# A gated attention and maxout kernel: one group of scores transposed instead of computed twice, and a new order in the first sequence's fourth step

## The chip, the cores and the metric

The kernel runs on one core of a Trainium2 chip. TensorE (PE) multiplies matrices and writes to PSUM; VectorE (DVE) and ScalarE (ACT) take results out of PSUM; GpSimd (POOL) and SyncE (SP) issue transfers here, each in its own queue, and both queues share the core's 16 DMA engines. GpSimd's queue carries the loads, SyncE's the transposing transfers between places in SBUF and the stores of the output. Each engine works through its own list of instructions in order and waits on semaphores of the others. The metric is the time on the device in microseconds (us), as a median over runs.

## What is computed

Two functions in a row. The first is an attention without softmax, over 8 sequences of 3072 rows; the second a maxout layer over all 24576 rows.

```python
scores = scale * np.matmul(z, z.transpose(0, 2, 1))     # z: 8 x 3072 x 64
attn = np.maximum(scores, 0.0) ** 2
out = np.matmul(attn, v)                                # v: 8 x 3072 x 256
x = (u * out).reshape(24576, 256)
g = np.maximum(x @ w1, x @ w2)                          # w1, w2: 256 x 1024
y = g @ w_out                                           # w_out: 1024 x 256
```

The score matrix of a sequence is symmetric, since both of its factors are z. The kernel writes the maxout as max(x(w1 - w2), 0) + x w2, so that y = max(x(w1 - w2), 0) w_out + x (w2 w_out); the product w2 w_out is computed once and is called the fold (`fold_w2o`, line 172).

## The kernel before

**Tiles and steps.** The 3072 rows of a sequence are 24 blocks of 128, called k, in 6 groups of four. A step (b, s) makes the 512 output columns of group s of sequence b: it adds up 24 k's in two accumulators of PSUM (`xacc`, one for each half of the 256 values of v), two matmuls of 128x512 for each k (`attn`, line 260). There is one pair of accumulators, so a step can begin only when the `epilogue` (line 264) has taken the accumulators of the step before out of PSUM: VectorE multiplies them with the transposed u (`uT`) and writes xT, two instructions, one for each accumulator.

**Scores.** A score pair (`scores_pair`, line 204) computes two k's against 512 columns: two matmuls of 64x512 on two halves of the array, one Relu on ScalarE into `r_sb`, one square on VectorE into `a_sb`. Three pairs make a window (`scores_window`), whose score matmuls stand together in TensorE's list. Since the scores are symmetric, a block of scores from one step, transposed, serves a later step. `turn` (line 200) sends such a pair through a transposing transfer on SyncE's queue into `aT`; the diagonal group of a step is transposed within itself (`aD`). A k whose scores are a step's own is added by `add_own`, one whose scores came transposed from an earlier step by `add_early`.

**Which scores are computed twice.** `direct(b, i, j)` (line 186) says for which pairs of groups i < j the later step computes the scores itself instead of getting them transposed. Before, this holds in sequence 0 for all of groups 0 to 3. So the steps (0,0) to (0,3) have no transposed rows, and each has 12 pairs of its own.

**Order of the work.** The loop over steps (lines 441 to 495) writes a list `work`. An entry has a nominal time, a mark if it needs the PSUM buffers shared with the scores, a function, and the score tiles that it reads with the time by which they must have been begun. The maxout of a step lags three steps (`LAG`): the hidden layer `put_d` (line 431; four pieces of four matmuls, L74 with tile d_ps) and the output chunk `put_o` (two pieces, tile o_ps) stand in the list of a later step. In step (0,3), the first with such work, the variable `within` puts the hidden layer of step (0,0) ahead of the sixth own pair, and the fold (nominal 1800 ns) with the first output chunk ahead of the tenth. In the steps (0,0) to (0,3) the first and the last four k's are ordered by accumulator (`add_half`): all four for one accumulator, then all four for the other.

**Where the windows go.** Lines 498 to 545 group the tiles to windows and lay them from the last to the first, each at the latest free spot before its tiles are due and at least `GAP_FIRST` or `GAP` before the next window. A spot is free if no entry that shares PSUM ends less than 860 ns before it or begins less than 1700 ns after it.

**Transfers.** Lines 549 to 600 list transfers by a step's nominal begin plus some microseconds: u's load and its transpose (`turn_u`), z and v of the next sequence, the weights. The load of w_out is listed 9 us after the begin of step (0,2). Where a load is reached in the list, GpSimd first runs a `gate` (line 82): a copy of one element of the newest tile (`fresh`), so that the load is not issued before that tile is there. `keep_in_program_order` pins matmuls, SyncE's transfers, gates and loads to the order in which they are written.

Of the kernel before, what the change touches and what calls it, by code (L numbers as in the profile page):

```python
# [11 lines left out]
def kernel(  # L12
# [29 lines left out]
    G = 4  # L42
    WIN = 3
    GW = G * P
    NG = NSB // G
    KD = D // P
    KF = Dff // P
    LAG = 3
    NDIR = 3
# [88 lines left out]
    def make_uT(u_sb):  # L138
        uT = upool.tile([P, G, KD, P], bf16, name="uT")
        sp_dma(  # L140
            out=uT.rearrange("p t c q -> p (t c) q"),
            in_=u_sb.rearrange("p t d -> p (t d)"),
            transpose=True,
        )
        return uT
# [38 lines left out]


    def direct(b, i, j):
        return b == 0 and i < j <= NDIR


    def score(q, out_ps, j, k, s, q0, n):  # L190
# [13 lines left out]
    def scores_pair(b, s, k0):  # L204
        q = seqs[b]
        s_ps = mm_psum.tile([P, 2, GW], fp32, name="s_ps", tag="mm")
        for j in range(2):
            score(q, s_ps[:, j, :], j, k0 + j, s, 0, G)
        yield
        a_sb = apool.tile([P, 2, GW], bf16, name="a_sb")  # L210
        r_sb = apool.tile([P, 2, GW], bf16, name="r_sb", bufs=3)

        head = b == 0 and s == 0 and k0 < 10
        keep = pin if head else lambda ins: None
        if head and k0 in (2, 6):
            keep(nc.vector.tensor_single_scalar(out=r_sb, in_=s_ps, scalar=0.0, op=ALU.max))  # L216
        else:
            keep(nc.scalar.activation(r_sb, s_ps, AF.Relu))  # L218
        if head and k0 < 4:
            yield  # L220
        keep(nc.vector.tensor_mul(a_sb, r_sb, r_sb))  # L221
        gj = k0 // G
        if gj > s and not direct(b, s, gj):
            if (s, gj) not in q.T:
                q.T[s, gj] = tpool.tile([P, G, G, P], bf16, name="aT")
            turn(
                q.T[s, gj][:, ds(k0 - G * gj, 2), :, :].rearrange("p k q x -> p (k q) x"),
                a_sb.rearrange("p j q -> p (j q)"),
            )
        yield a_sb  # L230
# [123 lines left out]
    class Step:  # L354
        def __init__(self, b, s):
            self.b, self.s, self.q = b, s, seqs[b]
            self.xacc = None
            self.n = [0] * KD
            self.diag = not (b == 0 and s <= NDIAG)
            self.rows = ([None] if self.diag else []) + [  # L360
                k0
                for k0 in range(0, NSB, 2)
                if k0 // G > s or direct(b, k0 // G, s) or (k0 // G == s and not self.diag)
            ]
            self.early = [i for i in range(s) if not direct(b, i, s)]
            self.scored = {}
# [11 lines left out]
                self.n[dc] += 1  # L378
            attn(self.q, k, moving, self.xacc, dcs, n == 0, n == NSB - 1)

        def add_early(self, k):
            i, qb = divmod(k, G)
            self.add(k, self.q.T[i, self.s][:, :, qb, :])

        def add_own(self, k, dcs=range(KD)):
            self.add(k, self.scored[k - k % 2][:, k % 2, :], dcs)

        def add_half(self, ks, dc):
            for k in ks:
                self.add_own(k, [dc])  # L390

        def add_diag(self, j):
            self.add(G * self.s + j, self.scored[None][:, j, :, :])
# [26 lines left out]
    LAT_OWN, LAT_TURNED, LAT_DIAG = 2900, 9000, 10000  # L420

    def put(ns, shares, fn, reads=()):
        work.append((ns, shares, fn, reads))

    def put_early(st, ks):
        for k in ks:
            i = k // G
            rows = [((NG * st.b + i, k0), LAT_TURNED) for k0 in (G * st.s, G * st.s + 2)]
            put(432, False, lambda st=st, k=k: st.add_early(k), rows)

    def put_d(n):
        if n >= 0:
            for _ in range(KF // 2):
                put(864, True, steps[n].piece_d)

    def put_o(n, split=False):
        if n >= 0:
            for _ in range(G // 2):
                put(2180, True, lambda: steps[n].piece_o(split))

    for n, st in enumerate(steps):
        b, s = st.b, st.s
        if n:
            put(0, False, steps[n - 1].finish)
        put(0, False, st.begin if n else lambda: None, "begin")
        early = [G * i + j for i in st.early for j in range(G)]

        within = {}
        lat = LAT_OWN if n > LAG else 6 * 432
        if s == 0:  # L450
            put_o(n - LAG)
        elif s == NG - 1:
            put_d(n - LAG)
            put_early(st, early[: len(early) // 2])
            put_o(n - LAG)
            put_d(n - LAG + 1)
            put_early(st, early[len(early) // 2 :])
        elif early:
            put_d(n - LAG)
            put_early(st, early[:-2])  # L460
            put_o(n - LAG)
            put_early(st, early[-2:])
        elif n == LAG:
            within = {
                5: lambda: put_d(0),
                9: lambda: (put(1800, True, fold_w2o), put_o(0)),
            }
        own = [k0 for k0 in st.rows if k0 is not None]
        for i, k0 in enumerate(own):
            if i in within:  # L470
                within[i]()
            if not early and n <= LAG and i in ((0, 1) if n else ()) + (len(own) - 2, len(own) - 1):


                if i in (0, len(own) - 2):
                    ks = [own[i], own[i] + 1, own[i + 1], own[i + 1] + 1]
                    for dc in range(KD):
                        put(
                            864,
                            False,  # L480
                            lambda st=st, ks=ks, dc=dc: st.add_half(ks, dc),
                            [((n, own[i]), lat), ((n, own[i + 1]), lat)],
                        )
                continue
            for k in (k0, k0 + 1):
                put(432, False, lambda st=st, k=k: st.add_own(k), [((n, k0), lat)])
        if st.diag:
            for j in range(G):
                put(432, False, lambda st=st, j=j: st.add_diag(j), [((n, None), LAT_DIAG)])
# [50 lines left out]
    for w in reversed(range(len(windows))):  # L540
        limit = min([limit] + [due[r] for r in windows[w] if r in due])
        found = [i for i in spots if begins[i] <= limit]
        i = found[-1] if found else 0
# [11 lines left out]
    def plan(b, s, us, is_load, fn):  # L555
        transfers.append((start_of[b, s] + us * 1000, len(transfers), is_load, fn))

    def plan_load(b, s, us, fn):
        plan(b, s, us, True, fn)

    def fetch_u(b, s):
        seqs[b].u_sb[s] = load_u(b, s)

    def turn_u(b, s):
        seqs[b].uT[s] = make_uT(seqs[b].u_sb[s])

    def fetch_z(b):
        seqs[b].z_sb = load_z(b, [NSB])
        seqs[b].v = new_v()

    def turn_z(b):
        seqs[b].zT = make_zT(seqs[b].z_sb)

    def fetch_v(b, i):
        load_v(b, seqs[b].v, i * G, G)

    for n, st in enumerate(steps):
        b, s = st.b, st.s
        if n + 1 < len(steps):
            nx = steps[n + 1]  # L580
            plan_load(b, s, 2 if b == 0 else 4, lambda nx=nx: fetch_u(nx.b, nx.s))
        plan(b, s, 1, False, lambda b=b, s=s: turn_u(b, s))
        if s == 0 and b + 1 < B:
            c = b + 1
            if b == 0:
                z_at, zT_at = (3, 5), (4, 4)
                v_at = [(3, 9), (3, 14), (4, 0), (4, 5), (4, 9), (4, 13)]
            else:
                z_at, zT_at = (2, 9), (3, 12)
                v_at = [(3, 2), (3, 8), (3, 14), (4, 2), (4, 8), (4, 14)]  # L590
            plan_load(b, *z_at, lambda c=c: fetch_z(c))
            plan(b, *zT_at, False, lambda c=c: turn_z(c))
            for i, at in enumerate(v_at):
                plan_load(b, *at, lambda c=c, i=i: fetch_v(c, i))
# [89 lines left out]
```

## Time and profile before

| | |
|---|---|
| median of 3 runs | 981.85 us (981.44 to 981.95) |
| the profiled execution's own time | 981.29 us |
| its span, first to last instruction | 979.5 us |
| busy: TensorE matmul, weight loads | 968.7, 510.3 us |
| busy: VectorE, ScalarE, GpSimd | 432.2, 442.6, 77.7 us |
| score matmuls (s_ps), recorded | 696 |
| transposes of score tiles (aT<-a_sb) | 228, median 3.6 us to landing |
| load of w_out | 1, issued at 52.0 us, 7.9 us to landing |
| loads of v and of u | 48 each, median 5.9 and 5.3 us to landing |

The span is shorter than the execution's time by what lies around the program. A line of a group in the profile names the line of the kernel, the engine, the operation, what is written and read, the number of instructions and their durations. All matmuls go through one helper and have line L74, so they are told apart by the tile that they write: s_ps scores, xacc attention, d_ps hidden layer, w2o_ps fold, o_ps output. A matmul of 512 columns shows a duration of 379 ns from its issue to its end, while such matmuls follow each other more closely, since they overlap; a few records of matmuls are missing.

### The profile page before, as it was taken

The numbers are of one execution on the slowest core, as the hardware profiler recorded it, in microseconds if no ns is written. First come the engines' busy times: TensorE is split into PE (matmuls) and PEld (weight loads), VectorE is DVE, ScalarE is ACT, GpSimd is POOL, SyncE is SP. The second block draws the span as 40 slices with busy tenths as digits, with TensorE's granted clock in tenths as the row PEclk, the third lists the DMA queues.
The fourth block names the chain that finished last, engine by engine and source line by source line (L and its number), as shares of the span: only waits on it lengthen the run. The fifth ranks groups of instructions, "written<-read, shape, count | busy, mean of one in ns | idle before, by whom it ended". The sixth has DMA issues, their size and how long they took to land.

```text
span 979.5 us, 14514 instructions
## 1 busy us (share of the span) xinstructions
PE 968.7 (99%) x5662; PEld 510.3 (52%) x5743; DVE 432.2 (44%) x681; ACT 442.6 (45%) x500; POOL 77.7 (8%) x228
## 2 busy tenths in 40 slices
PE   9999999999999999999999999999999999999998
PEld 3355545555455554555545564455545555445556
DVE  6654444443544435433445334444345443554322
ACT  6853454334643355433554335533355433654322
POOL 2011000110001100010000100011000110000000
PEclk9999999999999999999999999999999999999999
DMA  9999599987999969897788979889778796796621
GB/s 151 171 161 187 103 182 150 164 149 123 175 160 144 155 123 177 150 170 128 151 156 144 179 119 157 148 153 181 135 147 149 136 187 127 149 161 118 109 66 65
DMA packets 378517, 143.46 MB, mean 146 GB/s; under 512 B 356944, under 2 KB 358608, under 8 KB 378448
## 3 DMA queue, kind: packets, MB, share of 16 engines
q1 hardware_dynamic: 361888, 112.78, 61.5%
q0 software_dynamic: 16560, 29.74, 21.6%
q8 instruction: 45, 0.74, 0.3%
q14 instruction: 24, 0.20, 0.1%
HBM read 59.77 MB, written 25.17 MB: 87 GB/s over the span
## 4 chain that ended last, share of the span: by engine, by line
PE 99%; issue 1%; DVE 0%; ACT 0%
PE xacc L74 52%; PE o_ps L74 21%; PE d_ps L74 17%; PE s_ps L74 8%; PE w2o_ps L74 0%; ACT r_sb L218 0%; DVE r_sb L216 0%; PE tpz L134 0%; DVE a_sb L221 0%; DVE o_sb L317 0%; DVE blank L333 0%
## 5 line engine op out<-in xcount | busy, mean ns | idle before, releaser
L74 PEld LDWEIGHTS <-v_sb 128*128 128x128 bf16 x2304 | 215.9, 98 | 277.7 <-issue 41.1
L218 ACT ACTIVATE r_sb<-s_ps 128x1024 bf16<-128x1024 f32 x258 | 248.6, 1023 | 111.4 <-PE s_ps L74 111.2
L221 DVE TENSOR_TENSOR a_sb<-r_sb 128x1024 bf16<-128x1024 bf16 x260 | 179.4, 691 | 212.9 <-ACT r_sb L218 208.9
L74 PE MATMUL xacc<-a_sb,v_sb 128*128 128x512 bf16 x997 | 231.3, 379 | 2.5 <-issue 0.2
L74 PE MATMUL xacc<-aT,v_sb 128*128 128x512 bf16 x912 | 216.5, 379 | 0.0
L74 PE MATMUL o_ps<-w_out_sb,g_sb 128*128 128x256 bf16 x1536 | 199.1, 273 | 0.0
L74 PE MATMUL d_ps<-xT,w_sb 128*128 128x512 bf16 x751 | 172.7, 379 | 0.9
L74 PEld LDWEIGHTS <-g_sb 128*128 128x128 bf16 x1536 | 149.9, 98 | 27.6
L292 ACT ACTIVATE g_sb<-d_ps 128x1024 bf16<-128x1024 f32 x96 | 98.3, 1024 | 138.8 <-PE d_ps L74 138.8
L292 DVE TENSOR_SCALAR g_sb<-d_ps 128x1024 bf16<-128x1024 f32 x96 | 117.4, 1223 | 84.7 <-PE d_ps L74 81.3
L323 ACT COPY o_sb<-o_ps 128x512 f32<-128x512 f32 x94 | 55.1, 586 | 178.2 <-PE o_ps L74 178.2
L268 DVE SCALAR_TENSOR_TENSOR xT<-xacc,uT 128x512 bf16<-128x512 f32 x96 | 62.0, 683 | 137.4 <-PE xacc L74 137.4
L74 PEld LDWEIGHTS <-w_sb 128*128 128x128 bf16 x768 | 75.1, 98 | 88.7
L74 PE MATMUL s_ps<-zT 64*128 64x512 bf16 (+3 forms) x696 | 89.2, 359 | 0.1
L246 ACT ACTIVATE r_sb<-s_ps 128x896 bf16<-128x896 f32 x44 | 40.3, 917 | 97.9 <-PE s_ps L74 97.9
L74 PE MATMUL xacc<-aD,v_sb 128*128 128x512 bf16 x331 | 79.9, 379 | 2.6 <-issue 2.2
L74 PE MATMUL o_ps<-W2o_sb,xT 128*128 128x256 bf16 x384 | 73.3, 273 | 0.0
L248 DVE TENSOR_SCALAR r_sb<-s_ps 128x384 bf16<-128x384 f32 x44 | 24.6, 558 | 95.3 <-PE s_ps L74 95.3
L74 PEld LDWEIGHTS <-zT 64*128 64x128 bf16 x696 | 27.3, 94 | 62.6 <-issue 50.5
L83 POOL COPY gate_sb<-g_sb 128x1 bf16<-128x1 bf16 x44 | 8.3, 188 | 407.8 <-DVE g_sb L292 238.5
L74 PEld LDWEIGHTS <-xT 128*128 128x128 bf16 x384 | 37.6, 98 | 4.3
L83 POOL COPY gate_sb<-a_sb 128x1 bf16<-128x1 bf16 x48 | 9.7, 202 | 271.8 <-DVE a_sb L221 271.8
(37 smaller groups left out, 143.3 us busy)
## 6 DMA issues: line engine op xcount, KB each, us to landing
out_dram<-o_sb SPq DMA_DIRECT2D x47, 512.0 KB, 4.1
v_sb<-in_v_dram POOLq DMA_DIRECT2D x48, 256.0 KB, 5.9
u_sb<-in_u_dram POOLq DMA_DIRECT2D x48, 256.0 KB, 5.3
aT<-a_sb SPq DMA_TRANSPOSE x228, 3.6
z_sb<-in_z_dram POOLq DMA_DIRECT2D x7, 384.0 KB, 7.5
aD<-aD SPq DMA_TRANSPOSE x132, 2.4
w_sb<-in_moe_w_dram POOLq DMA_DIRECT2D x2, 512.0 KB, 7.5
uT<-u_sb SPq DMA_TRANSPOSE x48, 4.3
```

Source lines behind the costliest of these rows:

```text
L74: pin(nc.tensor.matmul(*args, **kw))
L83: pin(nc.gpsimd.tensor_copy(gate_sb, tile_ap))
L218: keep(nc.scalar.activation(r_sb, s_ps, AF.Relu))
L221: keep(nc.vector.tensor_mul(a_sb, r_sb, r_sb))
L246: nc.scalar.activation(r_sb, s_ps[:, 0:7, :], AF.Relu)
L248: nc.vector.tensor_single_scalar(out=r2_sb, in_=s2_ps[:, 2:5, :], scalar=0.0, op=ALU.max)
L268: nc.vector.scalar_tensor_tensor(out=xT[:, dc, :].rearrange("p (t q) -> p t q", q=P), in0=xacc[dc].rearrange("p (t q) -> p t q", q=P), sca ...
L292: nc.any.tensor_single_scalar(out=g_sb[:, nb : nb + 2, :], in_=d_ps, scalar=0.0, op=ALU.max)
L323: nc.any.tensor_copy(o_sb[:, ds(2 * th, 2), :], o_ps[:, :, :D])
```

## The change

`direct` gets a third condition, j - i < 3, which excludes the one case i = 0, j = 3. Step (0,0) now transposes its pairs 12, 13 and 14, 15 by DMA, and step (0,3) reads its first four k's from these instead of computing the pairs 0, 1 and 2, 3.

Step (0,3) so has transposed rows and takes the form of the later steps: hidden layer of step (0,0), all transposed rows but two, fold, output chunk of step (0,0), last two transposed rows, own rows. `within` is gone. The order by accumulator stays at the first four k's of steps (0,1) and (0,2) and at the last four of steps (0,0) and (0,1).

The transposes of u for steps (0,1) to (0,3) are listed 3 us ahead of the step's nominal begin instead of 1 us after it. The six loads of v for sequence 1 are listed from 6 us into step (0,4) to 11 us into step (0,5), instead of from 9 us into step (0,3) to 13 us into step (0,4). The other transfers are listed as before.

```diff
--- before.py
+++ after.py
@@ -184,7 +184,7 @@
 
 
     def direct(b, i, j):
-        return b == 0 and i < j <= NDIR
+        return b == 0 and i < j <= NDIR and j - i < 3
 
 
     def score(q, out_ps, j, k, s, q0, n):
@@ -378,16 +378,16 @@
                 self.n[dc] += 1
             attn(self.q, k, moving, self.xacc, dcs, n == 0, n == NSB - 1)
 
-        def add_early(self, k):
+        def add_early(self, k, dcs=range(KD)):
             i, qb = divmod(k, G)
-            self.add(k, self.q.T[i, self.s][:, :, qb, :])
+            self.add(k, self.q.T[i, self.s][:, :, qb, :], dcs)
 
         def add_own(self, k, dcs=range(KD)):
             self.add(k, self.scored[k - k % 2][:, k % 2, :], dcs)
 
         def add_half(self, ks, dc):
             for k in ks:
-                self.add_own(k, [dc])
+                (self.add_early if k // G in self.early else self.add_own)(k, [dc])
 
         def add_diag(self, j):
             self.add(G * self.s + j, self.scored[None][:, j, :, :])
@@ -422,11 +422,22 @@
     def put(ns, shares, fn, reads=()):
         work.append((ns, shares, fn, reads))
 
+    def reads_of(st, k, lat):
+        n, i = NG * st.b + st.s, k // G
+        if i in st.early:
+            return [((n - st.s + i, k0), LAT_TURNED) for k0 in (G * st.s, G * st.s + 2)]
+        return [((n, k - k % 2), lat)]
+
     def put_early(st, ks):
         for k in ks:
-            i = k // G
-            rows = [((NG * st.b + i, k0), LAT_TURNED) for k0 in (G * st.s, G * st.s + 2)]
-            put(432, False, lambda st=st, k=k: st.add_early(k), rows)
+            put(432, False, lambda k=k: st.add_early(k), reads_of(st, k, 0))
+
+
+
+    def put_border(st, ks, lat):
+        reads = sum((reads_of(st, k, lat) for k in ks), [])
+        for dc in range(KD):
+            put(864, False, lambda dc=dc: st.add_half(ks, dc), reads)
 
     def put_d(n):
         if n >= 0:
@@ -444,9 +455,9 @@
             put(0, False, steps[n - 1].finish)
         put(0, False, st.begin if n else lambda: None, "begin")
         early = [G * i + j for i in st.early for j in range(G)]
-
-        within = {}
+        own = [k for k0 in st.rows if k0 is not None for k in (k0, k0 + 1)]
         lat = LAT_OWN if n > LAG else 6 * 432
+
         if s == 0:
             put_o(n - LAG)
         elif s == NG - 1:
@@ -455,35 +466,24 @@
             put_o(n - LAG)
             put_d(n - LAG + 1)
             put_early(st, early[len(early) // 2 :])
-        elif early:
+        elif n >= LAG:
             put_d(n - LAG)
             put_early(st, early[:-2])
+            if n == LAG:
+                put(1800, True, fold_w2o)
             put_o(n - LAG)
             put_early(st, early[-2:])
-        elif n == LAG:
-            within = {
-                5: lambda: put_d(0),
-                9: lambda: (put(1800, True, fold_w2o), put_o(0)),
-            }
-        own = [k0 for k0 in st.rows if k0 is not None]
-        for i, k0 in enumerate(own):
-            if i in within:
-                within[i]()
-            if not early and n <= LAG and i in ((0, 1) if n else ()) + (len(own) - 2, len(own) - 1):
-
-
-                if i in (0, len(own) - 2):
-                    ks = [own[i], own[i] + 1, own[i + 1], own[i + 1] + 1]
-                    for dc in range(KD):
-                        put(
-                            864,
-                            False,
-                            lambda st=st, ks=ks, dc=dc: st.add_half(ks, dc),
-                            [((n, own[i]), lat), ((n, own[i + 1]), lat)],
-                        )
-                continue
-            for k in (k0, k0 + 1):
-                put(432, False, lambda st=st, k=k: st.add_own(k), [((n, k0), lat)])
+        else:
+            ks = (early + own)[:G] if n else []
+            if ks:
+                put_border(st, ks, lat)
+            early, own = early[G:], own[len(ks) if not early else 0 :]
+            put_early(st, early)
+        tail = own[-G:] if n + 1 < LAG else []
+        for k in own[: len(own) - len(tail)]:
+            put(432, False, lambda st=st, k=k: st.add_own(k), reads_of(st, k, lat))
+        if tail:
+            put_border(st, tail, lat)
         if st.diag:
             for j in range(G):
                 put(432, False, lambda st=st, j=j: st.add_diag(j), [((n, None), LAT_DIAG)])
@@ -579,12 +579,12 @@
         if n + 1 < len(steps):
             nx = steps[n + 1]
             plan_load(b, s, 2 if b == 0 else 4, lambda nx=nx: fetch_u(nx.b, nx.s))
-        plan(b, s, 1, False, lambda b=b, s=s: turn_u(b, s))
+        plan(b, s, -3 if b == 0 and 0 < s <= LAG else 1, False, lambda b=b, s=s: turn_u(b, s))
         if s == 0 and b + 1 < B:
             c = b + 1
             if b == 0:
                 z_at, zT_at = (3, 5), (4, 4)
-                v_at = [(3, 9), (3, 14), (4, 0), (4, 5), (4, 9), (4, 13)]
+                v_at = [(4, 6), (4, 11), (4, 16), (5, 1), (5, 6), (5, 11)]
             else:
                 z_at, zT_at = (2, 9), (3, 12)
                 v_at = [(3, 2), (3, 8), (3, 14), (4, 2), (4, 8), (4, 14)]
```

## The prediction

> **What bounds the kernel now.** I read the page first (busy shares, granted clock, chain of what ended last), then busy time by stretches of the span, then the chain between 44 and 80 us, where the change reorders the work, then the tile that is loaded there, and last the timeline for the two engines that decide when it arrives.
>
> ```profile
> span 979.5 us, 14514 instructions
> PE 968.7 (99%) x5662; PEld 510.3 (52%) x5743; DVE 432.2 (44%) x681; ACT 442.6 (45%) x500; POOL 77.7 (8%) x228
> PEclk9999999999999999999999999999999999999999
> PE 99%; issue 1%; DVE 0%; ACT 0%
> ```
>
> TensorE is busy all the time at full clock and nearly the whole chain is TensorE. So a saving off TensorE is worth nothing, a matmul taken away is worth its own time, and every microsecond that TensorE must wait is lost for good: no later slack gives it back. By stretches (us, then busy time of PE, PEld, DVE, ACT, POOL, then clock, share of the DMA engines, GB/s) the early part looks like the rest:
>
> ```profile
> 47.00:50.60 3.60, 3.60 (x21) 1.33 (x22) 3.49 (x5) 2.85 (x3) 0.00 (x0) 1.00 1.09 216
> 50.60:54.00 3.40, 3.35 (x18) 1.28 (x18) 2.91 (x6) 2.85 (x3) 1.08 (x2) 1.00 1.22 171
> 54.00:60.00 6.00, 6.00 (x32) 2.60 (x32) 3.90 (x5) 4.57 (x5) 1.69 (x6) 1.00 1.42 178
> ```
>
> TensorE has no hole, but the DMA engines are at or above full share, so transfers here land late. The chain through this stretch (start, length, what):
>
> ```profile
> 47.20 0.75 PE s_ps L74 x6
> 47.95 2.70 PE xacc L74 x12
> 50.65 0.75 PE s_ps L74 x6
> ...
> 56.69 3.45 PE d_ps L74 x16
> 60.14 1.73 PE xacc L74 x8
> ...
> 64.45 1.75 PE w2o_ps L74 x16
> 66.20 4.37 PE o_ps L74 x40
> ```
>
> Here a window of three score pairs and the 12 matmuls between two windows alternate every 3.45 us. Step (0,3) starts at about 50.6. The first step's hidden layer (d_ps) comes 6 us into it, the fold of the output weights (w2o_ps) at 64.3 to 64.5, the first output chunk behind that. The fold's operand (answer for w_out_sb):
>
> ```profile
> L74 PE MATMUL w2o_ps<-w_out_sb,w2T_sb x16: 272/272/273, 64.3 to 65.9; 128*128 128x256 bf16 x16
> L86 POOL DMA_DIRECT2D w_out_sb<-in_moe_w_out_dram x1: 894/894/894, 52.0 to 52.0; - x1
> DMA to landing us min/median/max: 7.9/7.9/7.9
> ```
>
> It is issued at 52.0, lands at 59.9 and is first read at 64.3: a slack of 4.4 us. What holds its issue is the gate on GpSimd, a copy that waits for the newest score tile (timeline):
>
> ```profile
> 50.74 0.68 DVE L221 TENSOR_TENSOR a_sb<-r_sb 128x1024 bf16<-128x1024 bf16 x1
> 51.56 0.18 POOL L83 COPY gate_sb<-a_sb 128x1 bf16<-128x1 bf16 x1 [9.49 <-DVE a_sb L221]
> 52.02 0.89 POOL L86 DMA_DIRECT2D w_out_sb<-in_moe_w_out_dram  x1 [0.28 <-issue]
> ```
>
> **The change, part by part.**
>
> *Scores removed.* Step (0,3) no longer computes pairs k 0, 1 and 2, 3: four score matmuls, two Relu, two squares. A period of 3.45 us holds 12 matmuls of 0.2157 (the 16 d_ps in 3.45 us) and three pairs, that is 4 x 0.2157. Laying the tiles out by the kernel's rule, 346 instead of 348, still gives 117 windows, so what a window costs beyond its pairs stays; two pairs at 0.2157 go: **-0.43 us**, on the path. The Relus (2 x 1.02) and squares (2 x 0.69) ran beside matmuls: 0.
>
> *Two transposes added on SP* in step (0,0), tiles (12, 13) and (14, 15), behind u's transpose, which is issued at 15.0 and lands at 21.8 (6.8 us). Their squares are ready about 15.0 and 15.9. Four such transposes took 9.94 us of SP from 16.87 to 26.81; six at that rate take 15, to about 31.3; by the 1.3 us of an issue that is not held up, to about 26. The next tile SP needs is ready at 30.4, so the queue is at most 1 us late there. Cover: these two tiles are wanted only in step (0,3), 54 us. u's transpose is ahead of them in its queue; its reader starts at 22.54 and the accumulator is wanted at 23.73, so it may be 1.2 us late before TensorE waits. I take 0; bounds 0 and 1.
>
> *u's transposes sooner.* Between old and new place of those of steps 1, 2 and 3 no other transposes are issued (the windows there hold tiles that are not turned), so SP issues in the same order. SP is in order and waits for u's load, which landed at 19.4, 32.1 and 46.6, earlier than SP gets there (26.9, 40.6, 52.1). Taken as 0; if u came late, the score transposes behind it would be late by as much.
>
> *v of the next sequence later*, on GpSimd behind its gates: six loads with 5.9 us to landing, moved from steps 3 and 4 to steps 4 and 5. The last is listed 9.5 us of list time ahead of sequence 1 and used 21 us after that begin; the first groups have longer. u's loads keep their order but for being passed by a v load of 0.5 us issue. 0; if the cover went, each late group would cost its lateness.
>
> *The order in step (0,3).* This is the part that counts. Before, step (0,3) had no transposed rows and put the hidden layer after ten k's, the fold after eighteen. Now it takes the common form: hidden layer (16 matmuls), k 0 and 1 (4 matmuls), fold, output chunk, k 2 and 3, own rows. No score window may lie in that stretch by the planner's 860/1700 rule. Up to the last matmul of step (0,2), at 50.58, TensorE has the same list as before. So the fold is reached at 50.58 + 16 x 0.2157 + 4 x 0.2157 = **54.9**, which is 9.4 us earlier than the 64.3 of before. Its other operands are there: w1's difference at 48.9, the transposed w2 at 48.6, the transposed scores long before.
>
> The load of w_out is not moved: still 9 us of list time into step (0,2), behind the same gate. 9.4 us sooner against a slack of 4.4: about 5.0 us late. Finer: the gate waits for the third square of the last window of step (0,2). Its Relu ends at 50.41, so the square can't end before 51.1 (issue 51.7); with the accumulators of (0,2) now finishing together, one evacuation of 0.68 ahead of it gives issue at 52.5, two 53.2. Landing: 7.9; the other two loads of that size (w1, w2) have a mean of 7.5, with 6.2 and 8.8 as ends. Ends of the stall: 51.7 + 6.2 - 54.9 = 3.0, and 52.5 + 8.8 - 54.9 = 6.4. I take one evacuation at half weight: 52.2 + 7.9 - 54.9 = **+5.2 us**. Behind the fold in TensorE's order stand the output chunk (which reads w_out too) and all else, so nothing fills the hole. Delays of k 0, of PSUM slots or of hidden-layer evictions vanish within it.
>
> The Trainium skill prices a GpSimd DMA lower (DMA: Bandwidth & Descriptors, section Anatomy of one DMA): about 2.0 us plus bytes over 436 GB/s. For 1.05 MB read that is an estimated 4.4 us, landing at 56.6, a stall of 1.7 and a sum near 983. The row of 7.9 us beside busy DMA engines decides against it.
>
> *The clock in the hole.* The first matmuls of the kernel ran slowly and later ones of the same form fast:
>
> ```profile
> 1.20 2.74 PE L74 MATMUL xacc<-blank 128*128 128x512 bf16 x6 [1.20 <-DVE blank L333]
> 4.70 1.03 PE L74 MATMUL xacc<-blank 128*128 128x512 bf16 x4
> ```
>
> 2.74 us for six against 1.03 for four: half speed for about 3.2 us, until about 4.4. At the end TensorE stops at 976.0 and the granted clock is still 1.00 up to 979.5, but its mean from 979.5 to 984 is 0.90. So an idle time of 3.5 us kept the clock there, and somewhat more loses it. A hole of 5.2 us may lose it; then up to 3.2 us at half speed cost up to 1.6. Bounds 0 and 1.6; neither row reaches 5.2 us, so I take the middle, **+0.8**.
>
> The skill's rule (TensorE: Matmul & The Clock Gate, Part 1: The HAM clock gate) is that one idle window of about 3.4 us halves the clock and one busy window restores it, the windows running freely. By that a hole of 5.2 us holds a whole window in about half of the runs, an estimate that agrees with the rows.
>
> *Tail of step (0,2) and ends of step (0,3)* no longer split by half: the hidden-layer matmuls that follow (3.45 us) cover the evacuations (2 x 0.68). 0. The window that now holds pair 22 with the next diagonal: before, such a window began at 78.70 and its square ended at 81.69, 3.0 us; TensorE gets to that k after 0.6 + 12 x 0.2157 = 3.2. 0, with 0.2 of margin.
>
> Sum: -0.43 + 5.2 + 0.8 = +5.6 on the profiled execution's 981.29 (979.5 of span, 1.8 around it) gives 986.9. The median shown is 981.85, 0.56 above that execution; on it, **987.4**.
>
> **Rivals.**
> 1. *The weights come in time* (ends on the other side). Mechanism: the load lands by the fold, and the removed scores are all that is left: 981.85 - 0.43 = 981.4. It decides when landing is under 57.3 (stall under 2.4). For it: the page's price, and the DMA engines lose the score transposes of 58 to 68. Against: none of the three loads landed in under 6.2 us, and the issue can't be before 51.7.
> 2. *A shorter stall*: landing nearer 6.2 us and the clock kept, stall 2.4 to 3.0: 983.8 to 984.4.
> 3. *A longer loss*: the clock stays halved for two stretches of 3.2 us (3.2 lost) with the 5.2 us: 981.85 - 0.43 + 5.2 + 3.2 = 989.8. For it: hardly more than the slow start; against: the start lasted one stretch.
> 4. *The transposes crowd the queue*, u of step 0 is over 1.2 us late and TensorE waits up to 1 us at 23.7: adds to the forecast, 988.4 in all. Against: u is first in its queue.
>
> **How the numbers follow.** Forecast 0.74 (with rival 4 counted in it, 0.08), rival 1 0.10, rival 2 0.07, rival 3 0.09. Low end: stall 3.0, no clock loss: 984.4. High end: stall 6.4 and 1.6: 989.4, and to 989.8 with rival 3. A measurement of this kernel tells about 0.2% (2.0 us) from no change. Faster by more would need a gain of 2.0 where 0.43 is in sight: 0.02. Within it lies rival 1, less a little: 0.09. Slower: 0.89.
>
> **What would show it.** TensorE idle once from about 54.9 to 60, the fold's first matmul released by the w_out load, and matmuls possibly at double spacing for 2 to 3 us after it; 692 score matmuls instead of 696; transposes aT 230 instead of 228; from sequence 1 on the same order, shifted by a constant. I would be wrong if w_out landed before 55, if the list puts the fold later than read here, or if an early u transpose stalled step (0,1).

## The result and the profile after

The changed kernel takes 989.54 us (median of 5 runs, 988.49 to 990.71) against 981.95 us (median of 5 runs) for the kernel before. The ratio is 1.007, with a 95% interval from 1.0046 to 1.0095: slower by 7.6 us, where the forecast was slower by 5.6 us (987.4, range 984.4 to 989.8). The profiled execution took 989.54 us, with a span of 987.8 us, 8.3 us more than the 979.5 us of before.

The head of the page, to be read against that of before:

```profile
span 987.8 us, 14513 instructions
PE 970.2 (98%) x5658; PEld 510.7 (52%) x5739; DVE 430.6 (44%) x679; ACT 441.0 (45%) x498; POOL 77.8 (8%) x228
PE 93%; issue 1%; DMA 1%; ACT 0%; DVE 0%; POOL 0%; DVEq 0%; ACTq 0%; POOLq 0%
L74 PE MATMUL s_ps<-zT 64*128 64x512 bf16 (+3 forms) x692 | 88.8, 359 | 0.1
aT<-a_sb SPq DMA_TRANSPOSE x230, 3.5
```

The work is as announced: 692 score matmuls recorded instead of 696, 230 transposes instead of 228. But the chain is no longer TensorE alone. From the fold it runs back into a DMA, and from there through GpSimd's gate, VectorE and ScalarE (chain between 44 and 90 us: start, length, what):

```profile
52.91 0.70 DVE a_sb L221
...
53.74 0.18 POOL gate_sb L83
53.93 0.28 issue
54.20 7.60 DMA w_out_sb<-in_moe_w_out_dram
61.80 0.14 issue
61.94 3.12 PE w2o_ps L74 x16
```

TensorE's waits name two places. The kernel before had neither; its only released wait on this list was the 1.2 us at its very start:

```profile
PE w2o_ps L74 <- DMA w_out_sb<-in_moe_w_out_dram: 4.6, 1, 4.6
PE xacc L74 <- DVE xT L268: 2.1, 2, 2.0
```

The first is the forecast one: the fold waits for its weights. The second was not forecast: at the end of step (0,1), VectorE could not take out the accumulators, since u's transpose had not landed. VectorE's timeline shows it, and SP's shows when that transpose was issued (start, length, engine, what, idle time before and what ended it):

```profile
38.88 0.69 DVE L268 SCALAR_TENSOR_TENSOR xT<-xacc,uT 128x512 bf16<-128x512 f32 x1 [2.39 <-DMA uT<-u_sb]
29.92 3.07 SPq L77 DMA_TRANSPOSE uT<-u_sb  x1
```

The same transpose of before, and the way to landing after and before (8.9 and 4.4 us; each is the only such transfer in its window):

```profile
26.86 1.31 SPq L77 DMA_TRANSPOSE uT<-u_sb  x1
DMA to landing us min/median/max: 4.4/4.4/4.4
```

```profile
DMA to landing us min/median/max: 8.9/8.9/8.9
```

It was issued 3.1 us later and took 4.5 us longer, and landed at 38.8 instead of 31.2 us (before, its reader on VectorE started at 36.34). VectorE had stood idle for it since 36.5 us.

The third loss is the clock. By stretches (busy times of PE, PEld, DVE, ACT, POOL, then the granted clock, share of the DMA engines, GB/s): TensorE is idle through the first stretch and works at half clock in the second, which is 3.4 us long.

```profile
57.30:61.90 4.60, 0.07 (x1) 0.00 (x0) 0.47 (x1) 0.00 (x0) 1.51 (x5) 1.00 1.31 191
62.44:65.86 3.42, 3.42 (x18) 2.38 (x17) 0.00 (x0) 0.74 (x2) 0.00 (x0) 0.50 0.55 107
```

So the ledger of the profiled execution closes on the three terms and the saving:

| term | how it is read | us |
|---|---|---|
| wait for u of step (0,1) | d_ps starts at 52.89 instead of the 50.58 where step (0,2) ended before | +2.3 |
| wait for w_out | fold starts at 61.94; reached at 52.89 + 20 x 0.2157 = 57.20 | +4.7 |
| half clock | 3.42 us at 0.50 | +1.7 |
| four score matmuls fewer | 2 x 0.2157, since two of them run side by side on the two halves of the array | -0.4 |
| sum | against the difference of the spans, 987.8 - 979.5 | 8.3 against 8.3 |

Nothing is lost later: the last matmul of all ends 8.4 us later than before. The mean clock of all five timed runs was 0.997 or 0.998, where the profiled execution of before had 1.000. That fits a loss of clock in each of them; how long it lasted is known for the profiled one alone.

### The profile page after: what moved, and what is told of

Read it like the earlier page. It is cut to its first block, busy times and chain, and to the rows that moved or that the text cites. A ratio compares the mean times of both kernels' runs of the same rounds, so it can differ in the third digit from the quotient of the medians.

```text
span 987.8 us, 14513 instructions
## 1 busy us (share of the span) xinstructions
PE 970.2 (98%) x5658; PEld 510.7 (52%) x5739; DVE 430.6 (44%) x679; ACT 441.0 (45%) x498; POOL 77.8 (8%) x228
## 3 DMA queue, kind: packets, MB, share of 16 engines
q1 hardware_dynamic: 364000, 113.30, 60.8%
## 4 chain that ended last, share of the span: by engine, by line
PE 93%; issue 1%; DMA 1%; ACT 0%; DVE 0%; POOL 0%; DVEq 0%; ACTq 0%; POOLq 0%
PE xacc L74 48%; PE o_ps L74 21%; PE d_ps L74 16%; PE s_ps L74 7%; DMA w_out_sb<-in_moe_w_out_dram 1%; ACT r_sb L218 0%; PE w2o_ps L74 0%; DVE a_sb L221 0%; DVE xT L268 0%; DVE o_sb L317 0%; POOL gate_sb L83 0%; DVEq L221 0%; ACTq L218 0%; POOLq L83 0%
## 5 line engine op out<-in xcount | busy, mean ns | idle before, releaser
L268 DVE SCALAR_TENSOR_TENSOR xT<-xacc,uT 128x512 bf16<-128x512 f32 x96 | 61.8, 684 | 126.2 <-PE xacc L74 114.8
```

The source lines that it names most:

```text
L268: nc.vector.scalar_tensor_tensor(out=xT[:, dc, :].rearrange("p (t q) -> p t q", q=P), in0=xacc[dc].rearrange("p (t q) -> p t q", q=P), sca ...
```

## The experiments

The theory from this profile: three losses with two causes. The fold overtook its load (wait and clock), and the two added transposes pushed u's transpose of step (0,1) into the time of w1's load. The rival throughout: the DMA engines are simply full between 16 and 60 us, and taking away one wait only moves it.

**The load of w_out sooner.** The changed kernel with

```diff
-    plan_load(0, 2, 9, lambda: load(out=w_out_sb, ...
+    plan_load(0, 2, 1, lambda: load(out=w_out_sb, ...
```

> The changed kernel with the load of w_out listed 1 us into step (0,2) instead of 9 us; nothing else differs. The changed kernel's ledger against the kernel before is: about 2.3 us of waiting for u's transpose of step (0,1), 4.7 us of waiting for w_out ahead of the fold, 1.7 us at half clock behind it, -0.4 for the removed scores. Theory (the fold overtook its load, and the clock was lost in that hole): both of the middle terms go, some 6.4 us less than the changed kernel, so about +1.9 us on the kernel before. TensorE then has no wait at the fold, and the granted clock is 1.00 throughout. Rival (the DMA engines are the bound in this stretch, and the load only crowds something else): the wait moves to the transposed w2, to u or to the score transposes, and the time stays at +4 us or more on the kernel before.

Measured: median 982.86 us against 982.27 for the kernel before, ratio 0.999, interval 0.995 to 1.0031. In the profiled execution (983.15 us) the fold follows the four matmuls of k 0 and 1 without a gap, and the wait for u alone is left (TensorE's timeline, then its waits):

```profile
56.37 1.03 PE L74 MATMUL xacc<-aT,v_sb 128*128 128x512 bf16 x4
57.23 1.91 PE L74 MATMUL w2o_ps<-w_out_sb,w2T_sb 128*128 128x256 bf16 x16
```

```profile
PE xacc L74 <- DVE xT L268: 1.9, 2, 1.7
```

The load now took 8.1 us from 43.2 us on and landed at 51.3, 6 us ahead of the fold. So the wait and the slow stretch both come from the load standing too late, and the DMA engines had room for it earlier: the theory holds. Of the +1.9 that was expected, the median shows 0.6 and the profiled execution all (a span of 981.4 against 979.5 us, 0.3 of it from a slower start). Two of the ten timed runs lie higher, at 986.86 and 990.21 us with a mean clock of 0.998 and 0.996; they were not profiled, and what they met is open.

**u's transpose of step (0,1) sooner.** The changed kernel with

```diff
-    plan(b, s, -3 if b == 0 and 0 < s <= LAG else 1, ...
+    plan(b, s, -7 if (b, s) == (0, 1) else -3 if b == 0 and 0 < s <= LAG else 1, ...
```

> The changed kernel with u's transpose of step (0,1) listed 7 us ahead of that step instead of 3, so that it stands in SP's queue behind three of the six score transposes of step (0,0) instead of behind all six. Theory (the two added transposes pushed it back in the queue, into the time of w1's load): it lands at about 28 to 30 us instead of 38.8, TensorE's wait of some 2.3 us at step (0,1)'s end goes, the rest of the loss stays: 2.3 us less than the changed kernel, about +5.3 to +5.9 on the kernel before. Rival (u's transpose is late because of the loads on the DMA engines, wherever it stands in the queue, or another transfer takes its place as the late one): no gain, +7.6 as in the changed kernel.

Measured: 988.48 us against 982.27, ratio 1.0069 (1.0053 to 1.0085). That is 6.2 us over the kernel before, where the changed kernel was 7.6 over: 1.4 less by the medians, not 2.3, and the two intervals overlap almost wholly, so that even this gain is not shown. The wait for u is gone (issued at 22.7, 6.3 us to landing). But in the profiled execution, the slowest of the four, the wait at the fold grew by almost the same amount (TensorE's waits, then the landing of w_out):

```profile
PE w2o_ps L74 <- DMA w_out_sb<-in_moe_w_out_dram: 6.7, 1, 6.7
```

```profile
L86 POOL DMA_DIRECT2D w_out_sb<-in_moe_w_out_dram x1: 892/892/892, 51.8 to 51.8; - x1
DMA to landing us min/median/max: 9.7/9.7/9.7
```

w_out was issued 2.4 us sooner and took 2.1 us longer, so it landed at 61.5 instead of 61.8. And the clock was at half for 6.8 us, some 4.1 of them with TensorE at work:

```profile
58.92:65.75 6.83, 4.08 (x20) 2.86 (x21) 0.00 (x0) 0.74 (x2) 0.00 (x0) 0.50 0.98 116
```

Here the rival is half right: with an earlier place in the queue u lands in time, but while the load of w_out stands where it is, a gain ahead of it can be given back at the fold, as it was in this execution.

**Both moves.** The edits of the two runs above together.

> The changed kernel with both moves: w_out's load 1 us into step (0,2), and u's transpose of step (0,1) 7 us ahead of it. Theory: all three losses go, and what is left is the removed scores, -0.4 us on the kernel before, to be seen in the span's windows though hardly in the median. Rival (the two transposes and the sooner load crowd the DMA engines between 16 and 55 us): a new wait of 1 us or more on TensorE before 60 us, time above the kernel before by that.

Measured: 981.19 us against 982.27, ratio 0.9994, interval 0.9984 to 1.0003. TensorE's waits are those of the kernel before, and 0.2 us more at the very start (the third line, which the changed kernel has too):

```profile
PE xacc L74 <- issue: 2.4, 15, 0.2
PE xacc L74 <- DVE blank L333: 1.2, 1, 1.2
PE tpz L134 <- DVE z_sb L343: 0.2, 1, 0.2
```

All that was lost is accounted for by the places of two transfers. What remains of the change, 0.4 us by the working, is too small to be told from nothing by these times. The two profiles show it: from the first attention matmul on scores (8.18 us before, 8.75 here) to the start of the last output matmuls (975.74 and 975.88) TensorE needs 967.56 us before and 967.13 here, 0.43 less.

**The hole filled with work.** The changed kernel with 20 matmuls of zeros ahead of the fold:

```diff
+    def keep_busy():
+        o = mm_psum.tile([P, GW], fp32, name="blank_ps", tag="mm")
+        for _ in range(20):
+            matmul(o, blank[:, :P], blank, start=True, stop=True)
...
+                put(0, False, keep_busy)
                 put(1800, True, fold_w2o)
```

> The changed kernel with 20 matmuls on a tile of zeros, 4.3 us of TensorE, put ahead of the fold; their result is not read. They fit into the hole of 4.7 us. Theory (the hole costs twice: by its length and by the clock that is lost in it): the wait for w_out stays, the clock stays at 1.00, and the 1.7 us behind it go: about +5.9 on the kernel before. Rival (the slow stretch behind the hole is not due to the idle time): no change, +7.6, or more if the blanks reach past the landing.

Measured: 986.96 us against 982.27, ratio 1.0051 (1.0033 to 1.0069): 4.7 us over the kernel before instead of 7.6, though TensorE does 4.3 us more. The clock stays at 1.00 and the fold runs at full speed, 1.91 us for its 16 matmuls instead of 3.12:

```profile
56.56 4.48 PE L74 MATMUL blank_ps<-blank 128*128 128x512 bf16 x20
60.88 1.91 PE L74 MATMUL w2o_ps<-w_out_sb,w2T_sb 128*128 128x256 bf16 x16
```

So the slow stretch behind the hole is due to TensorE's idle time. But TensorE did not wait for w_out any more, and the gain is larger than the 1.7 of the theory. In this execution the wait for u was 1.2 instead of 2.1 us and w_out took 6.3 instead of 7.6 us, landing at 59.9, so that the blanks even reached 1 us past it.

**The two transposes alone.** The kernel before; two tiles of step (0,0) are also transposed, into a spare tile:

```diff
+        if (b, s) == (0, 0) and k0 in (12, 14):
+            if k0 == 12:
+                spare[0] = tpool.tile([P, G, G, P], bf16, name="aT")
+            turn(spare[0][:, ds(k0 - 12, 2), :, :]..., a_sb...)
```

> The kernel before with only the two transposes added: tiles (12, 13) and (14, 15) of step (0,0) are also sent through SP's queue, into a tile that nothing reads; scores, order and listings are those of before. Theory (six transposes instead of four push u's transpose of step (0,1) into the time of w1's load): it lands at 38 to 39 us instead of 31.2, TensorE waits 1.2 to 2.4 us at the end of step (0,1), nothing else changes, since w_out's slack of 4.4 us covers it: +1.2 to +2.4 us on the kernel before. Rival (the lateness comes from the new listing or from the order of step (0,3), not from the queue): no change.

Measured: 983.49 us against 981.71, ratio 1.0009 (0.9978 to 1.0039). The median is 1.8 us higher, within the +1.2 to +2.4 that was expected, but the interval holds 1; the profile decides. u's transpose of step (0,1) is issued at 31.1 us, lands 7.5 us later, and TensorE waits for it, as it never did before (L277 is the epilogue's line in this kernel):

```profile
PE xacc L74 <- DVE xT L277: 1.2, 2, 1.1
```

It landed at 38.6, as expected, and there is no wait at the fold. The added transposes by themselves cause the wait at step (0,1). The rest of this execution's longer span (981.6 against 979.5) comes mostly from a start that was 0.8 us slower.

**The listings alone.** The kernel before with the new times of u's transposes and of v's loads, and nothing else.

> The kernel before with only the two changes of the listing: u's transposes of steps (0,1) to (0,3) listed 3 us ahead of the step instead of 1 us after it, and the loads of v for sequence 1 listed in steps (0,4) and (0,5). Theory (SP's queue keeps its order, and v has tens of us to spare): no change, within 0.5 us of the kernel before. Rival (SP waits on u's load earlier and holds up the transposes behind it, or the later v loads crowd sequence 1's first transposes): +1 us or more, with a wait in the profile that names uT or v_sb.

Measured: 982.16 us against 981.71, ratio 1.0003 (0.9993 to 1.0013). SP's list of transfers is the same, entry for entry, as in the kernel before, u's transpose of step (0,1) takes 4.7 us to landing, and no wait names u or v. These two parts of the change do nothing, as forecast.

**w1's load later.** The changed kernel with

```diff
-    plan_load(0, 1, 3, lambda: load(out=w1_sb, ...
+    plan_load(0, 1, 7, lambda: load(out=w1_sb, ...
```

> The changed kernel with w1's load listed 7 us into step (0,1) instead of 3 us, some 5 us later on the clock. This tells the two halves of the first wait apart: the later issue in SP's queue (29.9 instead of 26.9 us) and the longer way to landing (8.9 instead of 4.4 us) beside w1's load. Theory (the load makes the larger part): u's transpose of step (0,1) lands at about 35 us or sooner and TensorE's wait at the end of step (0,1) goes. As in the run with u's transpose sooner, the wait for w_out then grows by most of what was gained, so the time falls by 0 to 2.3 us, to +5.3 to +7.6 on the kernel before. Rival (the queue alone): it still lands after 37.5 us and the wait stays above 1 us.

Measured: 988.44 us against 981.71, ratio 1.007 (1.0055 to 1.0085). u's transpose keeps its late place in the queue, but w1's load is issued at 35.2 instead of 31.1 us:

```profile
30.37 3.19 SPq L77 DMA_TRANSPOSE uT<-u_sb  x1
DMA to landing us min/median/max: 5.3/5.3/5.3
```

5.3 us to landing instead of 8.9, landed at 35.7, no wait for u. The late place in the queue hurts only because of what it meets there. By the medians the kernel is 6.7 us over the kernel before instead of 7.6, and again the intervals overlap. In the profiled execution, the fastest of the four, little is given back: 4.8 us of waiting at the fold, where the changed kernel had 4.6, and 3.4 us at half clock as there; its span is 986.0 us, 1.8 less than the changed kernel's, behind a start that was half a microsecond slower. The other three were not profiled; two of them have a lower mean clock, 0.996 and 0.997 against 0.998.

**The order alone.** The kernel before, all scores computed as there, with the hidden layer and the fold of step (0,3) ahead:

```diff
-                5: lambda: put_d(0),
-                9: lambda: (put(1800, True, fold_w2o), put_o(0)),
+                0: lambda: put_d(0),
+                1: lambda: (put(1800, True, fold_w2o), put_o(0)),
```

> The kernel before with only the order of step (0,3) changed: hidden layer of step (0,0), first four k's, fold, output chunk, and then the other own rows. All scores are still computed, no transpose is added, the listings are those of before. Theory (the fold overtakes its load whatever else is changed): TensorE reaches the fold at about 56.6 us, w_out lands near 60.8, a wait of about 4.2 us at the fold and none at the end of step (0,1); with the clock kept +4.2 us on the kernel before, with a slow stretch of 3.4 us up to +5.9. Rival (the wait at the fold needs the other parts of the change): less than 1 us.

Measured: 990.21 us against 981.71, ratio 1.0086 (1.0069 to 1.0104), by the medians even more than the whole change, though the intervals overlap. TensorE's waits and the slow stretch:

```profile
PE w2o_ps L74 <- DMA w_out_sb<-in_moe_w_out_dram: 4.2, 1, 4.2
```

```profile
61.69:68.52 6.83, 5.47 (x26) 3.81 (x27) 0.00 (x0) 0.75 (x2) 0.00 (x0) 0.50 0.64 116
```

The wait is the 4.2 us that was expected, and there is none for u. That the size fits is in part luck: both its ends came over 2 us later than expected, the fold reached at 58.9 instead of 56.6 and w_out landed at 62.9 instead of 60.8. The clock stayed low for 6.83 us, 5.47 of them at work, which costs 2.7 us and not 1.7 at most. With 1.1 us in three short waits and a start that was 1.3 us slower (below) this makes 9.3 of the 9.9 us by which the span is longer; 0.6 stay open. The order alone is enough for the large part of the loss.

## Why the prediction was right, and where it was wrong

**The order in step (0,3): right.** The fold was reached 20 matmuls behind the end of step (0,2), as worked out, and waited for w_out: 4.6 to 4.7 us against 5.2 forecast. The run with the load sooner takes the wait away, and the run with the order alone brings it about. The way from issue to landing was 7.6 us where 7.9 was taken. The reading of slack against displacement (4.4 against 9.4 us) was the step that carried the forecast. Its accuracy owes something to luck: with u in time the wait was 6.7 us in one run, where w_out took 9.7 us, and 4.8 us in another, where it took 7.9. Why the same load takes from 6.3 to 9.7 us in these runs stays open.

**The clock in the hole: mechanism right, size too small.** The term was +0.8, the middle of 0 and 1.6; it measured +1.7 in the profiled execution. It lies just above the upper bound, which was taken from the 3.2 us of slow start; the stretches here are 3.4 us or twice that. The reading that 3.5 us of idle time keep the clock does not hold either: in the run with both moves TensorE stops at 976.3, and the clock falls at 978.3, 2.0 us later. What counts is how the idle time lies to a beat (last section). The Trainium skill's rule for the clock (TensorE: Matmul & The Clock Gate, Part 1: The HAM clock gate) agrees with the length of 3.4 us; that one busy window restores full speed fits as well, if a window only partly at work does not count as busy. But the window that cost the changed kernel its clock was not wholly idle: TensorE worked for 0.50 us in it.

**Two transposes added on SP: wrong.** The step took 0 with bounds 0 and 1, and measured +2.3. It had the queue 0 to 4.5 us later (3.1 measured), and u of step (0,0) safe, which it was. It then asked only when SP would next be needed for a *score* tile (30.4 us), and left out what stands in the queue ahead of that tile: u's transpose of step (0,1), issued at 26.9 before, with 5 us of slack at its reader. Three us later at issue still fits into that slack; what does not is the collision with w1's load, issued at 31.1: the way to landing grew by 4.5 us, and with w1's load later 3.6 of these are gone. The run with w1 later and the one with the transposes alone show both halves. Among its signs of being wrong the prediction had named a stall of step (0,1) by u's transpose, but by one that is early, not late, and at no price. Rival 4 had the right kind of wait at the wrong u and at under half the price.

**u's transposes sooner, and v later: right at 0.** SP's order is unchanged and the run with the listings alone is level with the kernel before.

**Scores removed: right.** The -0.43 closes the ledger at 8.3 us, and the run with both moves shows it in its profile, as 0.43 us less of TensorE's time.

**The rivals.** Rival 1 (weights in time) fell: issued at 54.2 us, w_out landed at 61.8. The 4.4 us that were estimated from the Trainium skill (DMA: Bandwidth & Descriptors, section Anatomy of one DMA) do not fit this stretch: w_out took 6.3 to 9.7 us in the runs here. Rival 3, the clock halved for two stretches, did not happen in the changed kernel's profile, but did in two of the experiments.

In sum, +5.6 was forecast on the profiled execution and +8.3 measured: 2.3 from a term that was taken as 0, 0.9 from the clock, less 0.5 at the fold. That 989.54 still lies within the range is luck: the upper ends of the sum's terms, 6.4 and 1.6, reach 989.4, and the last 0.4 of the range stands for rival 3, which is not what happened; the bound of 1 for the two transposes was not in it.

## What to carry to other kernels

When work is moved forward in the list of the engine that bounds the kernel, compare for each of its operands the distance of the move with the slack between landing and first use; the loads do not move along by themselves. When a transfer is added to an in-order queue, follow every transfer behind it, not just those of its own kind, to its reader, and ask what the later issue will collide with. Two late transfers in a row can hide each other: taking away the first wait alone returned 0.9 and 1.4 us of 2.3 by the medians, neither clear of noise, and in one of the two profiles nothing, since the next wait grew by as much.

## What the runs showed of the hardware that was not expected

The slow stretches come in one length or its double: 3.4 us in the changed kernel and with w1 later, 6.83 us with u sooner and with the order alone. The length of the hole does not decide it: 4.8 us of waiting (w1 later) cost one stretch, 4.2 us (order alone) two. What decides it is a beat. In all ten profiled executions the granted clock changes only at whole multiples of 3.413 us, counted from its first change to full speed: the changed kernel reaches full speed at 4.41, loses it 17 beats later at 62.44 and has it back one beat on, at 65.85. Taken beat by beat, TensorE's busy time orders all changes without an exception:

| beat of 3.41 us | TensorE at work in it, us | clock behind it |
|---|---|---|
| changed kernel, 55.61 to 59.03 | 1.76 | stays full |
| changed kernel, 59.03 to 62.44 | 0.50 | falls to half |
| w1 later, 56.63 to 60.04 | 0.00 | falls to half |
| w1 later, 60.04 to 63.45 | 3.06 | full again |
| u sooner, 58.92 to 62.33 | 0.66 | stays at half |
| order alone, 61.69 to 65.10 | 2.05 | stays at half |
| both moves, 974.89 to 978.30, the end | 1.37 | falls to half |

With w1 later the beat behind the fall was nearly all work:

```profile
60.04:63.45 3.41, 3.06 (x15) 2.22 (x16) 0.00 (x0) 0.37 (x1) 0.00 (x0) 0.50 1.30 117
```

In the two runs with 6.83 us it began with waiting, so a second beat at half clock followed, in which TensorE worked throughout. So where a hole falls against the beat sets its price. In these executions a beat with 1.37 us of work or less lost the clock and one with 1.76 or more kept it; a beat with 2.54 or less did not bring it back and one with 2.91 or more did. No run moved a hole on purpose, and where between these figures the limits lie is open.

A like effect shows at the very start. The kernel begins with slow matmuls, and the moment at which full speed comes differs from run to run: in the kernel before by the second group of blank matmuls, in the run with the listings alone after it (timelines of TensorE, before and then that run):

```profile
4.70 1.03 PE L74 MATMUL xacc<-blank 128*128 128x512 bf16 x4
```

```profile
4.98 1.91 PE L74 MATMUL xacc<-blank 128*128 128x512 bf16 x4
```

Same instructions, 1.03 against 1.91 us. That run's span was 980.9 us, 1.4 more than 979.5, with no wait that the kernel before does not have. The beat fits here too: the one from 0.98 to 4.39 us before had 3.09 us of work and full speed followed; the one from 0.32 to 3.73 in that run had 2.54 and it did not, so full speed came a beat later, at 7.14. From the first attention matmul on scores to the start of the last output matmuls both need 967.56 us. So differences of about 1 us between single executions of this kernel can come from the first 7 us alone.
